# RetNet attention and a tanh-shrink MLP on one core: the first eight steps as a list of one-engine pieces, zero matmuls in TensorE's pauses, other weight pieces, and one place per chunk for the attention

## The chip, the cores and the metric

The kernel runs on one core of a Trainium2 chip. The time is the device time of one execution in microseconds (us). Five engines run beside each other, each with its own queue in order: TensorE (PE; its weight loads are PEld), VectorE (DVE), ScalarE (ACT), GpSimd (POOL) and SyncE (SP), whose queue issues nearly all DMAs here.

## The reference

```python
def _attn_ref(q, k, v):                      # each (4, 8, 768, 64) float32
    gamma = 1.0 - 2.0 ** (-5.0 - np.arange(H))
    for t in range(S):
        state = gamma * state + k[:, :, t] outer v[:, :, t]
        y[:, :, t] = scale * (q[:, :, t] @ state)

def _moe_ref(x, w_in, w_out):                # x: y as (3072, 512)
    h = x @ w_in                             # w_in (512, 2048), float64 as given
    g = h - np.tanh(h)
    return (g @ w_out).astype(np.float32)    # w_out (2048, 512), float64 as given
```

Each head keeps a 64x64 state that decays and takes in one outer product per token. The result, 3072 tokens by 512, goes through an MLP with g = h - tanh(h).

## The kernel before

*Attention.* Tokens go in 24 chunks of 128 (6 per batch). Per chunk: `load_chunk` issues three DMAs (k, q, v); `scale_chunk` multiplies q and v by powers of gamma, so that the decay needs no loop; `turn` transposes k and q on TensorE (tile `kqTp`, 4 + 4 transposes) and `turn_copy` copies them out on ScalarE; `products` computes in 64x64 pieces (tile `s`) the new state parts k^T v and the scores, and VectorE masks the scores (`a`, line 261) and adds up the states (`state`, lines 268 to 274). `outputs` then forms y from states and scores in two halves. Between the halves ScalarE copies a few elements (`seen`, line 327), a wait by which no two 64x64 pieces write one place at once; after the second half, `rest`, ScalarE copies y into `xT` (line 331).

*Weights.* They come as float64 words and are made into float32 on the chip. They are loaded and converted in 32 pieces of 0.5 MB. `convert` has two steps on ScalarE, four on VectorE (lines 172 to 178) and two on POOL (179, 183; piece 1 on VectorE). A piece of w_in covers half the rows and 256 columns, so an `up` of 256 columns needs two.

*MLP.* 96 steps (n, m2): n is a block of 256 tokens, m2 a block of 256 of the 2048 columns. `up` (tile `h`, 8 matmuls in the code, 16 in the trace, since a float32 matmul appears as two), `shrink` (five operations on ScalarE, six on VectorE, giving `g`), `down` two steps later (LAG), 4 matmuls in the code and 8 in the trace, into `o`. The first 32 steps go through the weights in quarters (f) for n = 0 to 3, the rest through n = 4 to 11 whole.

*Order.* Nothing is reordered at run time: each engine takes its instructions as the program lists them. The first four steps and eight chunks are written out by hand at the end of the function, as calls that each touch several engines. A loop over steps 4 to 95 follows. In a step with a chunk, it does `outputs` of a chunk, then `up`, then `outputs_rest` and `products` of the next chunk, `shrink`, `downs`, and `turn`. PSUM: two tiles of two banks for transposes, scores and y (tag `t`), two banks for `h`, two for `o`. k, q and v have three buffers each.

Of the kernel before, what the change touches and what calls it, by code (L numbers as in the profile page):

```python
# [31 lines left out]
def kernel(  # L32
# [51 lines left out]
    def banks(name):  # L84

        return ps.tile([P, 2, BANK], F32, tag="t", name=name)
# [10 lines left out]
    seen = cst.tile([P, 2], F32, name="seen")  # L97

# [10 lines left out]
    room = [None]  # L109
    NW = 2 * NM  # L110

    def weight_ends(i):


        f, r = divmod(i, 2 * NC)
        if r < NC:
            c, cols = 2 * (r % 2), ds(BANK * f + TH * (r // 2), TH)

            return w1[:, ds(c, 2), cols], [
                (ds(0, P), 0, w_in[ts(c, P), cols]),  # L120
                (ds(0, D), 1, w_in[ds((c + 1) * P + D, D), cols]),
                (ds(D, D), 1, w_in[ds((c + 1) * P, D), cols]),
            ]
        m = NC * f + r - NC
        return w2[:, m], w_out[ts(m, P)]

    def load_weights(i):
# [4 lines left out]
        if w_out.dtype != F32:  # L132
            if 3 <= i < 9:

                if i % 2:
                    room[0] = xp.tile([P, 2, 2 * BANK], U32, tag="xT", name=f"raws_{i}")
                raw = room[0][:, (i + 1) % 2]
            else:
                raw = stage.tile([P, 2 * BANK], U32, tag="raw", name=f"raw_{i}", bufs=3)
            raws[i] = raw  # L140
        if not isinstance(src, list):
            if raw is None:
                nc.sync.dma_start(out=dst, in_=src)
            else:
                nc.sync.dma_start(out=raw, in_=src.bitcast(U32))
            return
        for r, k, w in src:
            if raw is None:
                nc.sync.dma_start(out=dst[r, k], in_=w)
            else:  # L150
                nc.sync.dma_start(out=raw[r, ts(k, BANK)], in_=w.bitcast(U32))

    def convert(i, engine=nc.gpsimd):
# [7 lines left out]

        if i not in raws:
            return
        dst, src = weight_ends(i)
# [3 lines left out]
        power = stage.tile([P, BANK], U32, tag="power", name=f"power_{i}", bufs=1)  # L168
        low = stage.tile([P, BANK], F32, tag="low", name=f"low_{i}")
        nc.scalar.activation(head.bitcast(F32), hi.bitcast(F32), AF.Abs)  # L170
        nc.scalar.activation(low, lo, AF.Copy, scale=2.0 ** -52)
        nc.vector.tensor_scalar(head.bitcast(F32), head.bitcast(F32), HI_MIN, HI_MAX,  # L172
# [5 lines left out]
        nc.vector.tensor_scalar(power, head, 0xFF800000, None, op0=ALU.bitwise_and)  # L178
        engine.tensor_tensor(low, low, power.bitcast(F32), op=ALU.mult)  # L179
        head = head.bitcast(F32)  # L180
        if isinstance(src, list):
            low, head = (t.rearrange("p (k n) -> p k n", k=2) for t in (low, head))
        engine.tensor_tensor(dst, low, head, op=ALU.add)  # L183

# [7 lines left out]
    def load_chunk(ci):  # L192
# [4 lines left out]
        for nm, src in (("k", k), ("q", q), ("v", v)):  # L197
            t = inp.tile([P, H, D], F32, tag=nm, name=f"{nm}_{ci}")
# [3 lines left out]
    def scale_chunk(ci, engine=nc.gpsimd):  # L202
        if ci >= NCH:
            return
        j = ci % CPB
        _, qh, vh = loaded[ci]
        for t, g in ((qh, gq), (vh, gv)):
            engine.tensor_tensor(  # L208
                t, t, g[:, ts(j, H)][:, :, None].to_broadcast([P, H, D]), op=ALU.mult
            )  # L210

    def turn(ci, tag="t"):

        if ci >= NCH:
            return
        if tag == "t":
            turned[ci] = [banks(f"kqTp_{ci}")]
        else:
            turned[ci] = [bank(tag, f"kqTp{i}_{ci}")[:, None] for i in range(2)]
        to = [t[:, i] for t in turned[ci] for i in range(t.shape[1])]  # L220
        for t, tp in zip(loaded[ci], to):
            for p in range(NP):
                nc.tensor.transpose(tp[:, ts(p, P)],  # L223
                                    t[:, ds(2 * p, 2)].rearrange("p h d -> p (h d)"), ident)

    def turn_copy(ci):
        if ci >= NCH:
            return
        t = mid.tile([P, 2, NP, P], F32, tag="kqT", name=f"kqT_{ci}")
        at = 0  # L230
        for tp in turned[ci]:
            n = tp.shape[1]
            nc.scalar.copy(out=t[:, ds(at, n)], in_=tp.rearrange("p i (n t) -> p i n t", n=NP))  # L233
            at += n
        turned[ci] = t

    def products(ci):

        if ci >= NCH:
            return
        kh, _, vh = loaded[ci]
        kT, qT = (turned[ci][:, i] for i in range(2))
        sp = banks(f"s_{ci}")
        halves = sp.rearrange("p r (w n t) -> p r w n t", w=2, n=NP)
# [6 lines left out]
        for p in range(NP):  # L253
            for a in range(2):
                for i in range(2):
# [3 lines left out]
                                     skip_group_check=True)  # L259
        m = mid.tile([P, 2, NP, D], F32, tag="a", name=f"a_{ci}")  # L260
# [3 lines left out]
        masked[ci] = m  # L264
        j = ci % CPB
# [10 lines left out]

    halfway = {}

    def outputs(ci):

        j = ci % CPB
        n, nj = divmod(ci, BLK)
        if nj == 0:
            xT[n] = xp.tile([P, NP, BLK * P], F32, tag="xT", name=f"xT_{n}")
        vh = loaded.pop(ci)[2]
        qT = turned.pop(ci)[:, 1]
        a_, st = masked.pop(ci), states.pop(ci)
        yT = banks(f"y_{ci}")
        y = yT[:, :, : 2 * P].rearrange("p r (n t) -> p r n t", n=2)
        begun = set()  # L290

        def to_y(p, i, a, lhsT, rhs):

            col = (i + p) % 2
            start = (p % 2, col) not in begun
            begun.add((p % 2, col))
            nc.tensor.matmul(y[ds(D * col, D), p % 2, p // 2, ts(a, D)], lhsT, rhs,  # L297
# [20 lines left out]
        intra(True)  # L318


        flat = yT.rearrange("p r w -> p (r w)")
        for col in range(2):
            r = ds(D * col, D)
            s0, s1 = 2 * P - 1 - D, BANK + 2 * P - 1
            if col:
                s0, s1 = 2 * P - 1, BANK + 2 * P - 1 - D
            nc.scalar.copy(out=seen[r], in_=flat[r, s0 : s1 + 1 : s1 - s0])

        def rest():
            intra(False)  # L330
            nc.scalar.copy(  # L331
                out=xT[n][:, :, ts(nj, P)].rearrange("p (n r) t -> p r n t", r=2), in_=y
            )

        halfway[ci] = rest

    def outputs_rest(ci):
        halfway.pop(ci)()
# [10 lines left out]
    def up(n, m2):  # L349
        hp = bank("h", f"h_{n}_{m2}")  # L350
        for i in range(2):
            for c in range(NC):
                nc.tensor.matmul(hp[:, ts(i, TH)], w1[:, c, ts(2 * m2 + i, P)],  # L353
                                 xT[n // 2][:, c, ts(n % 2, TH)], start=(i == 0 and c == 0),
                                 stop=(c == NC - 1), skip_group_check=True)
        hps[n, m2] = hp

    def shrink(n, m2):
        hp = hps.pop((n, m2))
        u, th, large = (work(x, 2) for x in ("u", "th", "large"))  # L360
        q0, q1 = (work(x, 1) for x in ("q0", "q1"))
        nc.scalar.activation(u, hp, AF.Square)  # L362
        nc.scalar.activation(th, hp, AF.Tanh)  # L363
        nc.scalar.activation(q0, u, AF.Square, bias=bias0)  # L364
        nc.scalar.activation(q1, u, AF.Square, bias=bias1, scale=math.sqrt(A))  # L365
        nc.scalar.activation(large, u, AF.Relu, bias=bias_m)  # L366
        nc.vector.tensor_tensor(th, hp, th, op=ALU.subtract)  # L367
# [230 lines left out]
```

## Time and profile before

| | |
|---|---|
| median of 3 runs | 786.57 us (785.92 to 788.78) |
| profiled execution | 788.5 us, its span 786.7 us |
| PE busy | 758.9 us (96%) |
| DVE, ACT, POOL busy | 522.2 (66%), 370.2 (47%), 123.7 us (16%) |
| HBM read, written | 35.80 MB, 6.29 MB |

The span is the stretch from the first instruction to the last; the profiled execution's own time has 1.8 us more around it. Busy times are shares of the whole span, over a start with loads and conversions and a long stretch of matmuls alone; what limits a stretch is read from that stretch. "Idle before" is an engine's pause, with what ended it behind the arrow. The granted clock is TensorE's: 1.00 full, 0.50 half.

### The profile page before, as it was taken

The numbers are of one execution on the slowest core, as the hardware profiler recorded it, in microseconds if no ns is written. First come the engines' busy times: TensorE is split into PE (matmuls) and PEld (weight loads), VectorE is DVE, ScalarE is ACT, GpSimd is POOL, SyncE is SP. The second block draws the span as 40 slices with busy tenths as digits, with TensorE's granted clock in tenths as the row PEclk, the third lists the DMA queues.
The fourth block names the chain that finished last, engine by engine and source line by source line (L and its number), as shares of the span: only waits on it lengthen the run. The fifth ranks groups of instructions, "written<-read, shape, count | busy, mean of one in ns | idle before, by whom it ended". The sixth has DMA issues, their size and how long they took to land.

```text
span 786.7 us, 13754 instructions
## 1 busy us (share of the span) xinstructions
PE 758.9 (96%) x5504; PEld 511.9 (65%) x5504; DVE 522.2 (66%) x808; ACT 370.2 (47%) x661; POOL 123.7 (16%) x106
## 2 busy tenths in 40 slices
PE   4869999999999999999999999999999999999997
PEld 4645776677667667666666666666666666666664
DVE  4676698789888875575666565566565656655654
ACT  3453566665655654443344444344444433444432
POOL 1155354333544441000000000000000000000000
PEclk9778999999999999999999999999999999999999
DMA  9953364443433422010000000000000000000000
GB/s 203 260 123 68 87 159 118 123 110 95 120 97 95 105 45 68 29 54 1 1 27 1 0 27 1 1 27 0 13 14 1 27 1 0 27 0 1 28 0 27
DMA packets 85711, 42.97 MB, mean 55 GB/s; under 512 B 76304, under 2 KB 76432, under 8 KB 85648
## 3 DMA queue, kind: packets, MB, share of 16 engines
q1 hardware_dynamic: 85504, 41.95, 21.2%
q8 instruction: 43, 0.70, 0.4%
q10 hardware_dynamic: 144, 0.15, 0.1%
q14 instruction: 20, 0.16, 0.1%
HBM read 35.80 MB, written 6.29 MB: 54 GB/s over the span
## 4 chain that ended last, share of the span: by engine, by line
PE 92%; DVE 4%; SPq 1%; issue 1%; ACT 1%; POOL 1%; DMA 1%; DVEq 0%; POOLq 0%; ACTq 0%
PE o L385 42%; PE h L353 42%; PE y L297 3%; PE kqTp L223 2%; PE s L257 1%; PE s L251 1%; SPq L199 1%; DVE head L176 1%; DVE head L174 1%; DMA raw<-in_moe_w_in_dram 1%; DVE a L261 0%; DVE power L178 0%; POOL low L179 0%; POOL w L183 0%; DVE head L172 0%
## 5 line engine op out<-in xcount | busy, mean ns | idle before, releaser
L385 PE MATMUL o<-w,g 128*128 128x512 f32 x768 | 351.8, 601 | 5.8 <-POOL w L183 5.3
L353 PE MATMUL h<-xT,w 128*128 128x256 f32 x1536 | 354.1, 384 | 3.0 <-POOL w L183 2.2
L353 PEld LDWEIGHTS h<-xT,w 128*128 128x128 f32 x1536 | 292.4, 192 | 71.8 <-issue 31.3
L385 PEld LDWEIGHTS o<-w,g 128*128 128x128 f32 x768 | 145.4, 192 | 152.6 <-issue 138.2
L362 ACT ACTIVATE u<-h 128x512 f32<-128x512 f32 x96 | 57.4, 598 | 268.6 <-PE h L353 268.6
L367 DVE TENSOR_TENSOR th<-h,th 128x512 f32<-128x512 f32 x96 | 66.2, 690 | 159.2 <-ACT th L363 159.2
L377 DVE COPY_PREDICATED g<-large,th 128x512 f32<-128x512 int32 x96 | 73.8, 769 | 10.6 <-DVE g L376 0.9
L370 DVE SCALAR_TENSOR_TENSOR h<-q,h 128x512 f32<-128x512 f32 x96 | 66.9, 697 | 10.4 <-DVE h L368 0.5
L372 DVE SCALAR_TENSOR_TENSOR h<-q,h 128x512 f32<-128x512 f32 x96 | 66.8, 696 | 10.0
L364 ACT ACTIVATE q<-u,tab 128x512 f32<-128x512 f32 x96 | 69.5, 724 | 0.0
L365 ACT ACTIVATE q<-u,tab 128x512 f32<-128x512 f32 x96 | 69.0, 719 | 0.0
L366 ACT ACTIVATE large<-u,tab 128x512 f32<-128x512 f32 x96 | 68.8, 716 | 0.0
L376 DVE TENSOR_TENSOR g<-h,u 128x512 f32<-128x512 f32 x96 | 66.3, 691 | 3.3
L368 DVE SCALAR_TENSOR_TENSOR h<-u,h 128x512 f32<-128x512 f32 x96 | 65.8, 685 | 0.0
L179 POOL TENSOR_TENSOR low<-low,power 128x512 f32<-128x512 f32 x31 | 39.6, 1277 | 157.4 <-DVE power L178 153.7
L363 ACT ACTIVATE th<-h 128x512 f32<-128x512 f32 x96 | 57.1, 594 | 0.0
L233 ACT COPY kqT<-kqTp 128x1024 f32<-128x1024 f32 (+1 forms) x28 | 24.8, 891 | 53.2 <-PE kqTp L223 53.0
L261 DVE TENSOR_TENSOR a<-s,tab 128x512 f32<-128x512 f32 x24 | 16.6, 690 | 41.5 <-PE s L257 41.4
L183 POOL TENSOR_TENSOR w<-low,head 128x512 f32<-128x512 f32 x31 | 39.8, 1283 | 2.4
L331 ACT COPY xT<-y 128x512 f32<-128x512 f32 x24 | 14.1, 587 | 53.5 <-PE y L297 53.5
L208 POOL TENSOR_TENSOR q<-q,tab 128x512 f32<-128x512 f32 x20 | 22.3, 1115 | 14.9 <-DMA q<-in_q_dram 14.9
L297 PEld LDWEIGHTS y<-kqT,state 64*64 64x64 f32 x704 | 12.9, 134 | 17.9 <-issue 11.7
(37 smaller groups left out, 372.2 us busy)
## 6 DMA issues: line engine op xcount, KB each, us to landing
k<-in_k_dram SPq DMA_DIRECT2D x24, 256.0 KB, 4.6
q<-in_q_dram SPq DMA_DIRECT2D x24, 256.0 KB, 5.1
v<-in_v_dram SPq DMA_DIRECT2D x24, 256.0 KB, 5.4
raw<-in_moe_w_out_dram SPq DMA_DIRECT2D x12, 512.0 KB, 3.7
out_dram<-sum SPq DMA_DIRECT2D x24, 256.0 KB, 2.0
raw<-in_moe_w_in_dram SPq DMA_DIRECT2D x14, 256.0 KB, 3.0
raw<-in_moe_w_in_dram SPq DMA_DIRECT2D x28, 128.0 KB, 4.2
raws<-in_moe_w_out_dram SPq DMA_DIRECT2D x4, 512.0 KB, 5.4
```

Of the source, the lines that this page charges most:

```text
L353: nc.tensor.matmul(hp[:, ts(i, TH)], w1[:, c, ts(2 * m2 + i, P)], xT[n // 2][:, c, ts(n % 2, TH)], start=(i == 0 and c == 0), stop=(c == N ...
L362: nc.scalar.activation(u, hp, AF.Square)
L364: nc.scalar.activation(q0, u, AF.Square, bias=bias0)
L365: nc.scalar.activation(q1, u, AF.Square, bias=bias1, scale=math.sqrt(A))
L366: nc.scalar.activation(large, u, AF.Relu, bias=bias_m)
L367: nc.vector.tensor_tensor(th, hp, th, op=ALU.subtract)
L368: nc.vector.scalar_tensor_tensor(hp, in0=u, scalar=R, in1=hp, op0=ALU.subtract, op1=ALU.mult, reverse0=True)
L370: nc.vector.scalar_tensor_tensor(hp, in0=q0, scalar=C0, in1=hp, op0=ALU.add, op1=ALU.mult)
L372: nc.vector.scalar_tensor_tensor(hp, in0=q1, scalar=A * C1, in1=hp, op0=ALU.add, op1=ALU.mult)
L376: nc.vector.tensor_tensor(flat, hp, u, op=ALU.mult)
L377: nc.vector.copy_predicated(flat, large.bitcast(I32), th)
L385: nc.tensor.matmul(o_p[j], gT[n, m2][:, i, ts(j, P)], w2[:, 2 * m2 + i], start=(first and i == 0), stop=(last and i == 1))
```

## The change

1. *The first eight steps* (before: four) are one string of pieces. Each piece is one engine's part of a former call, such as `p4` (scores and state products of chunk 4 on TensorE), `m4` and `z4` (mask, states, on VectorE), `A3`, `D3`, `G3` (conversion of piece 3 on ScalarE, on VectorE, and its end on POOL, or VectorE for pieces 0 and 1), `u2` and `v2` (the two halves of step 2's up), `o2` (its down). The string also holds chunks 0 to 7 and the conversions of 12 pieces.
2. *Zeros.* `x8` says: before the next TensorE piece, 8 matmuls of a 128x128 zero tile `busy`, into the place which that piece then overwrites. 47 in all, at 11 places.
3. *w_in by 128 columns and all rows*, so that a half `up` needs one piece; rows of 1 KB in DRAM, before 2 KB. Same bytes.
4. *Chunks in the loop:* every second step from 9 to 45 (before: 4 to 31). Rest of y, products of a chunk and first half of y of another stand in one row ahead of `up`; the transposes are at the step's end as before.
5. *Buffers.* y has a tile of its own of two banks, with two chunks in its halves; tag `t` keeps one tile of two banks for two. k and q have two buffers, v four. The early raw weights take three of the `xT` buffers. `power` has two buffers for one. `see` copies four single columns in place of two pairs.

Cut to its core:

```diff
+    busy = cst.tile([P, P], F32, name="busy")
+    nc.vector.memset(busy, 0.0)
...
-            c, cols = 2 * (r % 2), ds(BANK * f + TH * (r // 2), TH)
-
-            return w1[:, ds(c, 2), cols], [
...
+            cols = ts(NC * f + r, P)
+            rows = w_in[:, cols].rearrange("(k two p) n -> p two k n", two=2, p=P)
+
+            return w1[:, :, cols], [
...
+    def keep_busy(at):
+        for _ in range(idle[0]):
+            nc.tensor.matmul(at, busy, busy, start=True, stop=True, skip_group_check=True)
+        idle[0] = 0
...
-            t = inp.tile([P, H, D], F32, tag=nm, name=f"{nm}_{ci}")
+            t = inp.tile([P, H, D], F32, tag=nm, name=f"{nm}_{ci}", bufs=4 if nm == "v" else 2)
...
+    y_banks = banks("y", "y").rearrange("p r (two n t) -> p two r n t", two=2, n=2)
...
+    BEGUN = 8
+    EARLY_TURNS = 4
+    TO_VECTOR = 2
...
+    order = """
+    L0 x8 t0 c0 s0 x5 T0 w0 L1 C0 x3 t1 W0 p0 c1 s1 m0 x2 T1 z0 W1 C1 w1 x3 b0 p1 e0 A0 r0
+    m1 z1 y0 A1 D0 L2 x4 b1 t2 e1 c2 G0 r1 s2 y1 D1 x3 T2 w2 L3 u0 C2 W2 p2 G1 s3 t3 m2 T3
+    w3 c3 v0 z2 C3 b2 A2 L4 p3 e2 W3 D2 a0 r2 s4 y2 w4 q0 W4 m3 z3 G2 x9 t4 b3 A3 d0 T4 e3
...
+    for piece in order.split():
+        pieces[piece[0]](int(piece[1:]))
...
+    with_chunk = {BEGUN + 2 * i + 1: FIRST - 3 + i for i in range(NCH - FIRST + 3)}
...
     for s in range(BEGUN, len(steps)):
...
-            scale_chunk(ci + 2)
-            outputs(ci)
...
+            if ci >= FIRST:
+                outputs_rest(ci)
+                keep_x(ci)
+            if FIRST <= ci + 2 < NCH:
+                products(ci + 2)
+                mask(ci + 2)
+                state(ci + 2)
+            load_chunk(ci + 4)
+            if FIRST <= ci + 1 < NCH:
+                outputs(ci + 1)
+                see(ci + 1)
```

What it does to the queues is shown at three places.

VectorE at the first conversion of weights (`head`, `power`, `low`), before, with the masks `a` and states of chunks 0 and 1 around it:

```order
L261 TENSOR_TENSOR a_168<-s_135,tab 128x512
L268 COPY state_170<-s_135 128x256
L274 TENSOR_TENSOR state_172<-s_135,state_170 128x256
L172 TENSOR_SCALAR head_187<-head_187 128x512
L174 TENSOR_SCALAR head_187<-head_187 128x512
L176 SCALAR_TENSOR_TENSOR head_187<-raw_104,head_187 128x512
L178 TENSOR_SCALAR power_188<-head_187 128x512
L261 TENSOR_TENSOR a_251<-s_218,tab 128x512
L270 TENSOR_TENSOR state_172<-s_218,state_172 128x256
L274 TENSOR_TENSOR state_254<-s_218,state_172 128x256
```

and now:

```order
L234 TENSOR_TENSOR v_135<-v_135,tab 128x512
L299 TENSOR_TENSOR a_273<-s_224,tab 128x512
L311 TENSOR_TENSOR state_197<-s_224,state_197 128x256
L315 TENSOR_TENSOR state_276<-s_224,state_197 128x256
L179 TENSOR_SCALAR head_261<-head_261 128x512
L181 TENSOR_SCALAR head_261<-head_261 128x512
L183 SCALAR_TENSOR_TENSOR head_261<-raw_146,head_261 128x512
L185 TENSOR_SCALAR power_284<-head_261 128x512
L193 TENSOR_TENSOR low_262<-low_262,power_284 128x512
L197 TENSOR_TENSOR w_92<-low_262,head_261 128x4x128
```

The conversion of piece 0 moved behind the states of chunk 1, and its last two operations, to `w`, came over from POOL.

TensorE around the transposes of chunk 4 (`kqTp_638`) and the second up, before:

```order
L353 MATMUL h_1_579<-xT_198,w_90 128x256 x8
L353 MATMUL h_0_629<-xT_198,w_90 128x256 x8
L223 MATMUL kqTp_638<-tab,k_329 128x128 x4
L223 MATMUL kqTp_638<-tab,q_331 128x128 x4
L385 MATMUL o_0_0_666<-w_91,g_0_576 128x512 x2
L385 MATMUL o_0_1_669<-w_91,g_0_576 128x512 x2
L251 MATMUL s_672<-v_333,k_329 64x64 x16
L257 MATMUL s_672<-kqT_647 64x64 x16
L223 MATMUL kqTp_727<-tab,k_500 128x128 x4
L223 MATMUL kqTp_727<-tab,q_502 128x128 x4
```

and now (chunk 4 is `kqTp_543`, then `s_617`):

```order
L210 MATMUL kqTp_543<-busy 128x128 x9
L248 MATMUL kqTp_543<-tab,k_463 128x128 x4
L340 MATMUL y<-kqT_425,state_432 64x64 x16
L340 MATMUL y<-a_536,v_364 64x64 x8
L248 MATMUL kqTp_543<-tab,q_465 128x128 x4
L340 MATMUL y<-a_536,v_364 64x64 x8
L210 MATMUL s_617<-busy 128x128
L286 MATMUL s_617<-v_467,k_463 64x64 x16
L292 MATMUL s_617<-kqT_596 64x64 x16
L402 MATMUL h_0_656<-xT_278,w_92 128x256 x8
L402 MATMUL h_1_680<-xT_278,w_92 128x256 x4
```

The transposes moved ahead of that up, into chunk 3's y, behind nine zero matmuls; the next up is in halves, and no down comes before chunk 4's scores.

TensorE in the loop, from one chunk's y to the next transposes, before:

```order
L297 MATMUL y_1397<-kqT_1254,state_1213 64x64 x16
L297 MATMUL y_1397<-a_1350,v_1068 64x64 x8
L353 MATMUL h_1_1437<-xT_762,w_90 128x256 x8
L297 MATMUL y_1397<-a_1350,v_1068 64x64 x8
L251 MATMUL s_1455<-v_1219,k_1215 64x64 x16
L257 MATMUL s_1455<-kqT_1393 64x64 x16
L385 MATMUL o_0_0_1378<-w_91,g_1_1235 128x512 x2
L385 MATMUL o_0_1_1381<-w_91,g_1_1235 128x512 x2
L223 MATMUL kqTp_1523<-tab,k_1355 128x128 x4
L223 MATMUL kqTp_1523<-tab,q_1357 128x128 x4
```

and now:

```order
L340 MATMUL y<-a_1670,v_1382 64x64 x8
L286 MATMUL s_2008<-v_1679,k_1675 64x64 x16
L292 MATMUL s_2008<-kqT_1948 64x64 x16
L340 MATMUL y<-kqT_1763,state_1673 64x64 x16
L340 MATMUL y<-a_1855,v_1529 64x64 x8
L402 MATMUL h_5_2093<-xT_278,w_92 128x256 x8
L450 MATMUL o_2_0_1991<-w_93,g_3_1930 128x512 x2
L450 MATMUL o_2_1_1994<-w_93,g_3_1930 128x512 x2
L248 MATMUL kqTp_2123<-tab,k_1860 128x128 x4
L248 MATMUL kqTp_2123<-tab,q_1862 128x128 x4
```

The rest of y and the products, which stood behind the up, are ahead of it, in one row with the first half of the next chunk's y.

More of the change, by code (lines that the diff above doesn't have):

```diff
@@ L226, in turn_copy @@
[L226 to L235, printed above, removed]
+        t, g = loaded[ci][1 + which], (gq, gv)[which]
+        engine.tensor_tensor(t, t, g[:, ts(ci % CPB, H)][:, :, None].to_broadcast([P, H, D]),
+                             op=ALU.mult)
@@ new lines, with turn_copy, turn_chunk @@
+    sides = {}
+    def turn_copy(ci, which=None):
+        if ci not in sides:
+            sides[ci] = mid.tile([P, 2, NP, P], F32, tag="kqT", name=f"kqT_{ci}")
+        t = sides[ci]
+        if which is None:
+            nc.scalar.copy(out=t, in_=turned[ci].rearrange("p i (n t) -> p i n t", n=NP))
+        else:
+            nc.scalar.copy(out=t[:, which],
+                           in_=turned[ci][which].rearrange("p (n t) -> p n t", n=NP))
+    def turn_chunk(ci):
+        if ci < NCH:
+            turn(ci, 0)
+            turn(ci, 1)
+            turn_copy(ci)
@@ L264, in products, with state @@
         masked[ci] = m
+    def state(ci):
+        halves = scores.pop(ci)
         j = ci % CPB
@@ L386, in down, with add_up @@
                              start=(first and i == 0), stop=(last and i == 1))
-        if not last:
-            return
+    def add_up(n, m2, j):
         done = 2 * m2 + 2 == NM
```

346 lines of the change are left out of this document (167 added, 179 removed).

## The prediction

> **What bounds the kernel now.** I read the clock and busy time by stretches first, then TensorE's waits, then the chain that ended last, then the timeline of one chunk. In the first view each row is a stretch of the span: its length, the busy time of PE, PEld, DVE, ACT and POOL (with counts), the granted clock, the DMA share and GB/s. The cuts lie where the granted clock changes. The last row is of the timeline: start, length, instruction, and in brackets the pause before it.
>
> ```profile
> 0.00:11.43 11.43, 5.70 (x80) 4.80 (x80) 2.79 (x5) 2.88 (x4) 0.20 (x4) 1.00 1.05 198
> 18.26:25.09 6.83, 4.70 (x42) 3.72 (x42) 5.76 (x9) 0.89 (x3) 0.48 (x1) 0.50 0.78 217
> 35.33:45.57 10.24, 7.50 (x47) 5.37 (x37) 8.71 (x14) 5.06 (x11) 4.34 (x4) 0.50 1.03 236
> 52.39:55.80 3.41, 0.00 (x0) 0.00 (x0) 3.15 (x6) 3.05 (x6) 1.79 (x2) 1.00 0.00 0
> 55.80:62.63 6.83, 6.02 (x28) 2.46 (x32) 2.12 (x3) 0.00 (x0) 3.21 (x3) 0.50 0.01 2
> 69.46:72.87 3.41, 1.82 (x84) 1.48 (x74) 3.31 (x6) 2.84 (x6) 2.10 (x3) 1.00 0.56 128
> 72.87:76.29 3.42, 3.42 (x5) 1.31 (x5) 3.07 (x5) 0.82 (x4) 3.42 (x4) 0.50 0.61 112
> 0.00:98.86 98.86, 75.30 (x1248) 55.39 (x1249) 62.30 (x105) 45.89 (x88) 35.20 (x34) 0.86 0.65 149
> 4.87 1.09 PE L223 MATMUL kqTp<-tab,k 128*128 128x128 f32 x4 [4.87 <-DMA k<-in_k_dram]
> ```
>
> Up to 98.86 us TensorE is busy for 75.30, so 23.6 us are pauses. Four stretches have half the clock; their busy time is 4.70 + 7.50 + 6.02 + 3.42 = 21.6 us, and the first 11.43 us, though shown as 1.00, run at half speed too (the four transposes of the last row take 1.09 us there; the same form takes 0.60 in the row of 191.75 below), with 5.70 busy: half of 27.3, 13.7 us, is lost to the clock. Half clock follows stretches of 3.4 us in which TensorE was busy for 0.00 or 1.82, and full clock came back at 76.29, after 3.42 busy of 3.42. So the start loses 37 us, and after 76 us nothing is lost. TensorE's longest waits:
>
> ```profile
> PE o L385 <- POOL w L183: 5.3, 1, 5.3
> PE kqTp L223 <- DMA k<-in_k_dram: 4.9, 1, 4.9
> PE h L353 <- POOL w L183: 2.2, 1, 2.2
> ```
>
> The second cannot go; the others are late conversions of weights. After the start TensorE is the chain itself (start, length, piece):
>
> ```profile
> 334.59 3.45 PE h L353 x16
> ...
> 706.47 3.45 PE h L353 x16
> ```
>
> 54 steps lie between: 371.88 / 54 = 6.887 us a step, 3.45 up and 3.43 down, no gap. 96 steps make 661 us that this change does not touch.
>
> **The change, step by step.** I set up the sum as: when is the order string worked off on TensorE, and what is left then.
>
> *What is left, and how the formula does on the kernel before.*
>
> ```profile
> 98.86 3.70 PE L385 MATMUL o<-w,g 128*128 128x512 f32 x8
> 182.38 0.69 PE L297 MATMUL y<-kqT,state 64*64 64x64 f32 x32
> 183.24 3.72 PE L353 MATMUL h<-xT,w 128*128 128x256 f32 x16
> 186.89 0.46 PE L297 MATMUL y<-a,v 64*64 64x64 f32 x16
> 187.17 0.65 PE L251 MATMUL s<-v,k 64*64 64x64 f32 x32
> 187.64 0.65 PE L257 MATMUL s<-kqT 64*64 64x64 f32 x32
> 188.21 3.70 PE L385 MATMUL o<-w,g 128*128 128x512 f32 x8
> 191.75 0.60 PE L223 MATMUL kqTp<-tab,k 128*128 128x128 f32 x4
> 192.62 3.62 PE L353 MATMUL h<-xT,w 128*128 128x256 f32 x16
> ...
> 199.61 0.69 PE L297 MATMUL y<-kqT,state 64*64 64x64 f32 x32
> 777.56 5.42 PE L385 MATMUL o<-w,g 128*128 128x512 f32 x12 [0.51 <-DVE g L377]
> L331 ACT COPY xT<-y 128x512 f32<-128x512 f32 x24 | 14.1, 587 | 53.5 <-PE y L297 53.5
> ```
>
> Two steps with one chunk last 199.61 - 182.38 = 17.23 us, so a chunk costs 17.23 - 13.77 = 3.46. Its own pieces are y 0.86, rest of y 0.28, s 0.47 + 0.57, transposes 0.87: 3.05. The other 0.4 is paid by the neighbours: the up between two 64x64 pieces takes 3.65 (183.24 to 186.89) where the plain one takes 3.45, and the s before a down takes 0.57 for 0.47. With rest, s and y in one row, one such pair goes: 0.20 + 0.10. I take 3.15 a chunk, 16 x 0.31 = 5 us over chunks 8 to 23. No new wait covers it up: the first y matmul stands behind ScalarE's copy of the chunk before, 0.59 us long (L331), and 0.94 us of s lies between.
>
> At 98.86 before has done 6 ups, 3 downs, chunks 0 to 7, and 1.9 us of chunk 8. Left: 90 x 6.887 + 3 x 3.43 + 15 x 3.46 + 1.5 = 683.4; the end adds 0.5 (wait for the last g) and 3.7 (782.98, where that row's last matmul ends, to 786.7): 786.5, against a span of 786.7. The formula holds.
>
> After the order string 8 ups, 6 downs and chunks 0 to 7 are done. Left: 88 x 6.887 + 2 x 3.43 + 16 x 3.15 + 4.2 = 667.5. Before reaches that much work at 98.86 + 6.9 + 10.3 - 1.9 = 114.2.
>
> *When the string is done.* I walked it piece by piece, each starting when its engine and inputs are free. Four parts result, with these rows:
>
> ```profile
> 16.86 0.42 DVE L274 TENSOR_TENSOR state<-s,state 128x256 f32<-128x256 f32 x1
> 20.38 0.69 DVE L179 TENSOR_TENSOR low<-low,power 128x512 f32<-128x512 f32 x1
> ...
> 21.72 0.69 DVE L208 TENSOR_TENSOR q<-q,tab 128x512 f32<-128x512 f32 x1
> L174 DVE TENSOR_SCALAR head<-head 128x512 uint32<-128x512 uint32 x11 | 8.5, 772 | 0.4
> L176 DVE SCALAR_TENSOR_TENSOR head<-raw,head 128x512 uint32<-128x512 uint32 x5 | 4.4, 883 | 0.2
> 29.52 0.69 DVE L261 TENSOR_TENSOR a<-s,tab 128x512 f32<-128x512 f32 x1 [4.91 <-PE s L257]
> 30.58 0.42 DVE L274 TENSOR_TENSOR state<-s,state 128x256 f32<-128x256 f32 x1
> 66.97 0.42 DVE L172 TENSOR_SCALAR head<-head 128x512 f32<-128x512 f32 x1
> 67.42 1.38 DVE L174 TENSOR_SCALAR head<-head 128x512 uint32<-128x512 uint32 x1
> 68.84 1.64 DVE L176 SCALAR_TENSOR_TENSOR head<-raws,head 128x512 uint32<-128x512 uint32 x1
> 70.58 0.43 DVE L178 TENSOR_SCALAR power<-head 128x512 uint32<-128x512 uint32 x1
> 70.92 0.68 DVE L261 TENSOR_TENSOR a<-s,tab 128x512 f32<-128x512 f32 x1
> ```
>
> (a) To the states of chunk 1. Before they end at 17.3, with a conversion (2.0 on DVE) ahead of them. After, that is behind them, but zeros stand ahead of TensorE's first pieces. A zero matmul has half the columns of an up matmul pair (2 x 0.216 for 256): 0.22 us, at half clock 0.43. The first 8 lie in the 4.9 us wait; the 5 and 3 before the next transposes cost 3.4, of which waits of 0.8 and some for k cover half. The two cancel: 17.3.
>
> (b) DVE from there to the states of chunk 3: three conversions of 0.42 + 0.77 + 0.88 + 0.43 = 2.5 (the means of L174 and L176 up to 100 us, and L172 and L178 as at 66.97 and 70.58), two endings on DVE of 1.34 (20.38 to 21.72), two masks with states of 1.5 (29.52 to 31.00): 7.5 + 2.7 + 3.0 = 13.2, and 0.7 of hand-overs: 31.2. W_in by 128 columns is what lets the up of half a tile run beside it.
>
> (c) TensorE then: 9 zeros 1.9 (they wait for the bank that these states free), transposes 0.44, y 0.86, transposes 0.6, ScalarE's copy of 1024 columns 1.0 (estimated from L331's 0.587 for 512), one zero and hand-overs 0.5: s of chunk 4 at 36.5.
>
> (d) From there TensorE always finds work: 14 half ups of 1.73 = 24.2, 6 downs 20.6, four chunks' s, y and rest 4 x 2.18 = 8.7, transposes of chunks 5 to 7 2.6, 9 zeros 1.9: 58.0. End: 94.5. DVE ends 3 us after TensorE in the walk, so it is nearly a bound itself.
>
> I add 1.5, half of the 66.97 conversion's surplus on each of two: POOL is busy 35.2 of 98.86 us before with nine endings and twelve scalings, and in the walk has ten and twelve between 17 and 80, so conversions meet it more often than the mean of 2.5 contains. 96.
>
> ```profile
> 14.00:18.00 4.00, 1.49 (x54) 0.97 (x47) 3.83 (x9) 2.27 (x6) 1.87 (x2) 1.00 1.36 217
> 46.00:48.00 2.00, 2.00 (x11) 1.77 (x10) 0.71 (x2) 1.83 (x4) 1.92 (x3) 1.00 1.03 252
> ```
>
> *What I cost at nothing.* Loads: the trace has rows of 256 B (q, k, v, at 217 GB/s) and of 2 KB (w_in, at 252), none of 1 KB. Between them a piece of 0.524 MB takes 2.08 to 2.42 us. The walk's loads run one after another: chunk 4 lands at 28 to 31, for transposes at 33, the twelfth piece at 62. Two buffers for k and q put each k load, and all behind it in SP's queue, behind TensorE's s of two chunks earlier; that is early enough by 4 us. Four small copies of ScalarE per chunk for two: ScalarE is idle half the time. The memset of zeros: in the first wait.
>
> Sum: 96 + 667.5 = 763.5 us of span. The profiled execution (788.5 us, span 786.7) lies 1.9 above the median of 786.57, so the median stands where the span does: **764**.
>
> The trace shows a conversion of 2.0 us stretched to 3.95 (66.97 to 70.92) while POOL ends the conversion before. [...]
>
> **Rivals.** *Clock not held.* Zeros and 64x64 pieces do not count enough, and TensorE runs at half clock until the first long row of ups, at some 45 us. TensorE has 22.8 us of pieces between 11.4 and that row; doubled, they add 22.8, of which its pauses of 7.5 and the shorter rest take 10: end of string 108, time 776. For: 1.82 busy of 3.41 lost the clock. Against: in the walk no 3.4 us have over 1.2 us of pause. Chance 0.12.
>
> *DVE and POOL collide.* Each conversion takes 3.95: DVE is the bound from 17 us on, 12 x 1.45 = 17 more, of which some 6 fall into slack: 107, time 774. Halfway: 769. Chance of over 770 by this: 0.10.
>
> *Nothing gained, or slower.* The same clock mechanism beyond the first ups: the string breaks ups into halves with small pieces between, so if half clock lasts to 60 us, the string ends at 115, a draw; to its end, at 135, and the time is 802. Against: full clock came back after one dense stretch of 3.42. Draw 0.03, slower 0.03.
>
> *Better.* The first zeros bring full clock at 8 instead of 11.4 us (-1.5), and POOL hits no more than now (-1.5), a chunk costs 3.05 (-1.6): 759. Chance 0.15, and the forecast itself, 760 to 769, has 0.57.
>
> [...]
>
> **How the numbers follow.** 757 to 775 leaves out 0.03 below and, above, half of the first rival (0.06), the end of the second (0.03) and the two without a gain (0.06). Under 0.5% (3.9 us) no change could be told. Faster 0.94, same 0.03, slower 0.03.
>
> **What would show it.** Right: the granted clock stays at 1.00 from about 11 us on; the PE waits of 5.3 and 2.2 on POOL are gone; the last down of the string ends near 96; up halves of chunk steps take 3.46 and a chunk step pair 16.9; DVE over 90% busy from 40 to 95. Wrong: stretches of 0.50 after 15 us, PE waiting for DVE or POOL (g or w) after 37, or conversions of 3 us and more.

## The result, and the profile after

The changed kernel takes 768.06 us (median of 4 runs, 767.69 to 769.91), the kernel before 787.25 (785.92 to 788.78): a ratio of 0.976, 95% interval 0.9735 to 0.9785. The forecast was 764, 757 to 775. The profiled execution took 768.03 us, its span is 766.0, 20.7 shorter than before.

The first view is the one by stretches, of the changed kernel, cut where the granted clock changes (columns as in the prediction). The row 36.42 to 97.72 is part (d) of the walk, and at 97.72 the first up of the loop starts, so there the string is done.

```profile
0.00:6.14 6.14, 4.93 (x22) 4.67 (x23) 0.17 (x1) 1.30 (x2) 0.20 (x4) 1.00 0.85 156
...
12.97:16.38 3.41, 1.78 (x72) 1.51 (x64) 2.49 (x6) 2.17 (x6) 0.00 (x0) 1.00 1.17 212
16.38:19.79 3.41, 3.41 (x59) 2.99 (x57) 3.24 (x5) 1.49 (x6) 1.54 (x2) 0.50 1.04 217
...
36.42:97.72 61.30, 60.20 (x700) 42.43 (x700) 55.73 (x84) 38.97 (x80) 29.92 (x24) 1.00 0.49 125
0.00:97.72 97.72, 91.53 (x1327) 70.15 (x1328) 81.04 (x125) 57.34 (x122) 39.55 (x36) 0.98 0.69 156
```

One stretch of 3.41 us has half the clock where there were four of 27.3 together, and the start runs at full clock from 6.14 instead of 11.43. Up to 97.72 TensorE pauses for 6.2 us (97.72 - 91.53); it was 23.6. TensorE's waits after:

```profile
PE kqTp L210 <- DVE state L315: 2.6, 2, 1.5
PE y L210 <- ACT xT L381: 1.5, 1, 1.5
PE kqTp L210 <- DVE busy L99: 1.1, 1, 1.1
PE y L340 <- ACT xT L381: 0.7, 1, 0.7
```

The waits of 5.3, 4.9 and 2.2 us are gone. Line 210 is the zero matmul: it is the zeros that wait now. The 4.9 us for the first k are not shorter; 1.1 of them is the memset of the zeros (`busy`), and eight zeros fill the rest.

Two steps with a chunk, in TensorE's timeline after, to be set against the rows from 182.38 in the prediction:

```profile
219.18 0.46 PE L340 MATMUL y<-a,v 64*64 64x64 f32 x16
219.46 0.65 PE L286 MATMUL s<-v,k 64*64 64x64 f32 x32
219.93 0.65 PE L292 MATMUL s<-kqT 64*64 64x64 f32 x32
220.40 0.65 PE L340 MATMUL y<-kqT,state 64*64 64x64 f32 x32
220.87 0.41 PE L340 MATMUL y<-a,v 64*64 64x64 f32 x16
221.21 3.72 PE L402 MATMUL h<-xT,w 128*128 128x256 f32 x16
224.77 3.60 PE L450 MATMUL o<-w,g 128*128 128x512 f32 x8
228.20 0.60 PE L248 MATMUL kqTp<-tab,k 128*128 128x128 f32 x4
229.07 3.62 PE L402 MATMUL h<-xT,w 128*128 128x256 f32 x16
...
236.06 0.46 PE L340 MATMUL y<-a,v 64*64 64x64 f32 x16
```

236.06 - 219.18 = 16.88 us, so a chunk costs 16.88 - 13.77 = 3.11; before it was 3.46. The down that used to stand behind s took 3.54 from start to start (188.21 to 191.75), now 3.43.

Where the time of the string went can be added up: pauses as above; the clock's loss as half of the busy time in stretches at half clock, the start included; and zeros at 0.22 us each (24 of them take 5.36 in a row further on). Before, the same work is done at 114.2 by the prediction's formula.

| us | end of string | pauses | lost to the clock | zeros | the rest |
|---|---|---|---|---|---|
| before | 114.2 | 23.6 | 13.7 | 0 | 76.9 |
| changed | 97.7 | 6.2 | 4.2 | 10.3 (47) | 77.0 |
| changed, no zeros (first experiment below) | 98.6 | 14.0 | 8.7 | 0 | 75.9 |
| changed, first 21 zeros | 96.4 | 9.4 | 5.5 | 4.6 | 76.9 |
| best version (last but one experiment) | 94.2 | 8.4 | 1.7 | 5.7 (26) | 78.4 |

The rest is TensorE's own work. It is the same in the first two rows; over all rows it differs by 2.5, so the columns are good to about that (a row of y, for one, takes 1.13 us at half clock and 0.69 at full, so it loses less than half). The change gains 17.4 us of pauses and 9.5 of clock, and pays 10.3 of zeros. After the string 766.0 - 97.7 = 668.3 us are left, 672.5 before.

### The profile page after: what moved, and what is told of

It reads as the page before. It is cut to its first block, busy times and chain, and to the rows that moved or that the text cites. A ratio compares the mean times of both kernels' runs of the same rounds, so it can differ in the third digit from the quotient of the medians.

```text
span 766.0 us, 13968 instructions
## 1 busy us (share of the span) xinstructions
PE 754.9 (99%) x5598; PEld 517.1 (68%) x5598; DVE 524.5 (68%) x807; ACT 375.3 (49%) x709; POOL 124.3 (16%) x108
## 4 chain that ended last, share of the span: by engine, by line
PE 95%; DVE 2%; SPq 1%; DMA 1%; ACT 0%; issue 0%; DVEq 0%
PE h L402 43%; PE o L450 42%; PE y L340 3%; PE kqTp L248 3%; PE s L286 1%; PE s L292 1%; SPq L227 1%; DMA raw<-in_moe_w_in_dram 1%; PE kqTp L210 0%; DVE head L183 0%; SPq L152 0%; DVE head L181 0%; PE y L210 0%; DVE power L185 0%; DVE head L179 0%
## 5 line engine op out<-in xcount | busy, mean ns | idle before, releaser
L402 PE MATMUL h<-xT,w 128*128 128x256 f32 x1536 | 349.9, 381 | 0.0
L450 PE MATMUL o<-w,g 128*128 128x512 f32 x768 | 345.5, 593 | 0.5 <-DVE g L441 0.5
L402 PEld LDWEIGHTS h<-xT,w 128*128 128x128 f32 x1536 | 288.5, 190 | 62.9 <-issue 26.5
L441 DVE COPY_PREDICATED g<-large,th 128x512 f32<-128x512 int32 x96 | 75.4, 785 | 10.9 <-DVE g L440 1.4
L234 POOL TENSOR_TENSOR q<-q,tab 128x512 f32<-128x512 f32 x22 | 23.6, 1072 | 107.6 <-DMA q<-in_q_dram 101.9
L260 ACT COPY kqT<-kqTp 128x1024 f32<-128x1024 f32 x20 | 20.2, 1012 | 22.6 <-PE kqTp L248 22.4
L340 PEld LDWEIGHTS y<-a,v 64*64 64x64 f32 x768 | 16.1, 136 | 15.0 <-ACT large L421 11.4
L234 POOL TENSOR_TENSOR v<-v,tab 128x512 f32<-128x512 f32 x22 | 24.9, 1131 | 0.8 <-DMA v<-in_v_dram 0.8
L370 ACT COPY seen<-y 64x1 f32<-64x1 f32 x96 | 10.1, 154 | 24.8 <-PE y L340 24.4
```

The costliest lines, as they stand in the source:

```text
L402: nc.tensor.matmul(hp, w1[:, c, ts(2 * m2 + i, P)], xT[n // 2][:, c, ts(n % 2, TH)], start=(i == 0 and c == 0), stop=(c == NC - 1), skip_g ...
L441: nc.vector.copy_predicated(flat, large.bitcast(I32), th)
L450: nc.tensor.matmul(o_p[j], gT[n, m2][:, i, ts(j, P)], w2[:, 2 * m2 + i], start=(first and i == 0), stop=(last and i == 1))
```

## The experiments

Three questions were open: are the zeros or the order what shortens the start, what do the 128-column pieces and the one place in the loop bring, and what still holds the string up. Each run is set against runs of the kernel before on its own chip; these had medians of 786.87 (first four), 787.65 (next three) and 787.56 us (last three). Each kernel was timed four or five times; the stretches and rows are of one execution.

### All zeros out

```diff
-    L0 x8 t0 c0 s0 x5 T0 w0 L1 C0 x3 t1 ...
+    L0 t0 c0 s0 T0 w0 L1 C0 t1 ...            # and so on for all eleven groups
```

> All 47 zero matmuls left out, the rest of the changed kernel as it is. Theory A (the zeros hold the clock, and that is where much of the gain comes from): the trace after has one half-clock stretch of 3.4 us; without zeros there are three or more, as before, full clock comes at 11 us or later in place of 6.1, and the time is 5 to 10 us longer, 773 to 778. Theory B (the order does it; the zeros mostly run after the wait they are meant to fill, since they write into the place that the next piece waits for): 9 zeros at 30.8 us, 6 at 44.1, 1 at 36.0, 3 at 60.8 and 4 at 15.9 stand in the way for 2.1 + 1.4 + 0.4 + 0.7 + 1.6 us; without them the time is within 3 us of 768, and any half-clock stretch costs no more than the zeros did.

Measured: 769.57 us, ratio 0.9771 (0.9752 to 0.979). By the medians all 47 zeros are worth 1.5 us, which is not clear of the spread (768.02 to 770.05 here, 767.69 to 769.91 with them), and the other edits keep nearly the whole gain. The stretches of this run:

```profile
18.07:24.90 6.83, 5.78 (x49) 4.68 (x49) 6.59 (x7) 2.18 (x7) 3.71 (x4) 0.50 0.70 171
35.14:38.55 3.41, 0.46 (x16) 0.32 (x16) 3.20 (x6) 2.61 (x8) 1.65 (x2) 1.00 1.04 231
38.55:41.96 3.41, 3.33 (x67) 3.00 (x68) 2.10 (x4) 1.57 (x3) 2.73 (x3) 0.50 0.99 297
```

Zeros do keep the clock (without them 10.2 us at 0.50, and full clock at 14.66 for the first time), but they take nearly the time that they save: the table's 4.5 us of clock and 7.8 of pauses against 10.3.

### Only the first five groups of zeros

```diff
-    ... L2 x4 b1 ... D1 x3 T2 ... G2 x9 t4 ... y3 x1 p4 ... L6 x6 t5 ... C7 x3 u4 ...
+    ... L2 b1 ... D1 T2 ... G2 t4 ... y3 p4 ... L6 t5 ... C7 u4 ...
```

> Only the first five groups of zeros stay (8, 5, 3, 2 and 3, up to 11.9 us); the six later groups go. Theory A (later zeros hold the clock too): half-clock stretches after 16 us, 2 to 6 us longer than the changed kernel, 770 to 774. Theory B (the later groups run after their wait and delay what follows): the 2.1 us at 30.8, 1.4 at 44.1, 0.4 at 36.0 and 0.7 at 60.8 come back, 764 to 765, full clock from 6 us on but for at most one stretch near 16 us.

Measured: 766.91 us, 0.9738 (0.9721 to 0.9755). By the medians the later 26 zeros cost about 1.2 us, less than was expected; that is hardly clear of the spread (766.18 to 767.26 here, 766.28 to 768.00 in a later repeat of the changed kernel). The rows of the changed kernel show why they do not fill a pause, TensorE first:

```profile
30.77 2.25 PE L210 MATMUL kqTp<-busy 128*128 128x128 f32 x18 [1.47 <-DVE state L315]
32.86 0.60 PE L248 MATMUL kqTp<-tab,k 128*128 128x128 f32 x4
34.87 0.46 PE L340 MATMUL y<-a,v 64*64 64x64 f32 x16
44.06 1.57 PE L210 MATMUL kqTp<-busy 128*128 128x128 f32 x12 [1.09 <-DVE state L315]
```

The nine zeros write the place that VectorE reads for the states, so they wait 1.47 us with the transposes and then delay them by 2.1. Why removing them brings so little is seen in TensorE's timeline without the later zeros, and then in ScalarE's of the changed kernel:

```profile
35.29 0.46 PE L340 MATMUL y<-a,v 64*64 64x64 f32 x16 [2.33 <-ACT seen L370]
```

```profile
33.08 0.69 ACT L170 ACTIVATE head<-raws 128x512 f32<-128x512 f32 x1 [0.94 <-DMA raws<-in_moe_w_in_dram]
...
34.38 0.43 ACT L370 COPY seen<-y 64x1 f32<-64x1 f32 x4
```

ScalarE's part of conversion 3 (lines 170, 171) stands ahead of the look at y (`seen`) in its queue and waits for its load, so y cannot go on before 34.8 with zeros or without. The zeros do stand behind their wait, but a second wait lay in their shadow.

### w_in by 256 columns again

```diff
-            cols = ts(NC * f + r, P)
-            return w1[:, :, cols], [ ...
+            c, cols = 2 * (r % 2), ds(BANK * f + TH * (r // 2), TH)
+            return w1[:, ds(c, 2), cols], [ ...
```

Since half an up then needs two pieces, `u0` was moved to just ahead of `v0` and `u1` to just ahead of `v1`; nothing else.

> Pieces of w_in as before: 256 columns and half the rows, rows of 2 KB; since a half up then needs two pieces, the first half of step 0's up moves behind the second piece's conversion and that of step 1's behind the fourth's. Theory A (the 128-column pieces matter): the first up waits for the second piece, and TensorE's pauses near 22 and 44 us grow by 1.5 to 2 us each, 770 to 772. Theory B (TensorE was waiting for VectorE's chain of conversions and masks there, not for an up): within 1.5 us of 768.

Measured: 771.83 us, 0.9801 (0.9784 to 0.9818), 3.8 more than the changed kernel; the string ends at 101.42, and what follows takes 668.3 us as in the changed kernel. The row that pays:

```profile
44.53 2.90 PE L209 MATMUL kqTp<-busy 128*128 128x128 f32 x12 [2.52 <-DVE state L314]
```

Without a half up to put there, TensorE waits 2.52 us for the states where the changed kernel waits 1.09, and a stretch at half clock follows (44.25 to 47.67). Another 0.8 us is lost before: the products of chunk 4 start at 37.20 instead of 36.42. The edit undoes the pieces and the halves together, so the 3.8 us are theirs together.

### Two places per chunk in the loop

```diff
+        # ahead of up: outputs(ci + 1), see(ci + 1) only
         up(...)
+        # behind up: outputs_rest, keep_x, products(ci + 2), mask, state, load_chunk(ci + 4)
```

> In the loop the rest of y and the products go back behind the up, as before; the order string stays. Theory A (each chunk pays for its second excursion with 0.2 us in the up and 0.1 in the products): 16 chunks x 0.3 to 0.37 = 5 to 6 us longer, 773 to 774, two steps with a chunk 17.2 us in place of 16.87. Theory B (the pairs of form changes cost nothing by themselves; the difference came from elsewhere in the loop): within 1.5 us of 768.

Measured: 773.06 us, 0.9819 (0.9801 to 0.9837), 5.0 more. The string ends at 98.05, as it should, and what follows takes 771.5 - 98.05 = 673.4 us, 5.1 more than in the changed kernel. TensorE in this run:

```profile
222.24 0.69 PE L340 MATMUL y<-kqT,state 64*64 64x64 f32 x32
...
223.09 3.72 PE L402 MATMUL h<-xT,w 128*128 128x256 f32 x16
226.75 0.46 PE L340 MATMUL y<-a,v 64*64 64x64 f32 x16
...
239.46 0.69 PE L340 MATMUL y<-kqT,state 64*64 64x64 f32 x32
```

The pair takes 17.22 us, as before the change, and the up between the two excursions 3.66 (223.09 to 226.75) where in one row it takes 3.56 (221.21 to 224.77). So the loop's part of the gain is the one excursion itself: the term of 5 us held.

### Two orders mended on ScalarE and VectorE

The kernel with the first zeros, and three moves: the look at y and the copies of chunks 3 and 4 ahead of conversion 3 on ScalarE, the states of chunk 4 ahead of conversion 4 on VectorE, `b4` ahead of `v1` on TensorE.

```diff
-    ... G2 t4 b3 A3 d0 T4 e3 C4 r3 g0 L5 y3 p4 A4 ... m4 D4 u1 G3 a2 q2 z4 L6 ... v1 W7 C5 g2 b4 s6
+    ... G2 t4 b3 d0 T4 e3 C4 r3 g0 L5 y3 p4 A3 A4 ... m4 z4 D4 u1 G3 a2 q2 L6 ... b4 v1 W7 C5 g2 s6
```

> As the kernel with only the first five groups of zeros (766.9 us), and three pieces moved in the string: the look at y, the copy of the transposes and the copy of y of chunks 3 and 4 go ahead of piece 3's conversion on ScalarE, which waits there for its load; the states of chunk 4 go ahead of piece 4's conversion on VectorE; chunk 4's first y goes ahead of the second half of step 1's up. Theory A (queue order, not the clock, is what is left to gain: TensorE's wait of 2.3 us for the look at y at 35.3, and its wait for the states at 44 in the changed kernel): the products of chunk 4 start at 34 instead of 36.4, the string ends near 92 to 93, time 762.5 to 764. Theory B (VectorE's chain is the bound of the whole string and takes back what TensorE is given): 766 to 768.

Measured: 765.57 us, 0.9721 (0.9705 to 0.9738): by the medians 1.3 us less than the kernel with the first zeros (the two intervals overlap), but short of what was expected by about as much again. ScalarE now does the look at 32.18, 2.2 earlier:

```profile
32.18 0.43 ACT L370 COPY seen<-y 64x1 f32<-64x1 f32 x4
```

The products of chunk 4 start at 33.90, where they started at 36.42 with the first zeros alone and in the changed kernel too: so it was ScalarE's order that set this time. But the string ends at 95.22, not at 92 to 93, where it ended at 96.38 with the first zeros alone: of the 2.5 us half is lost again by then. TensorE's timelines of the two runs show where. At chunk 5's transposes this run is 4.1 us ahead (40.27 for 44.35), since its products came 2.5 us earlier and the other run has a stretch at half clock there (36.44 to 39.85). Then it waits, among others, twice for work of POOL and VectorE:

```profile
42.73 1.99 PE L402 MATMUL h<-xT,w 128*128 128x256 f32 x8 [0.56 <-POOL w L197]
46.54 3.72 PE L402 MATMUL h<-xT,w 128*128 128x256 f32 x16 [0.46 <-DVE g L440]
```

A wait of 0.52 us at 51.17 ends 0.1 after VectorE's states of chunk 5, and the down from 62.94 takes 4.29 to the next start where its neighbour takes 3.64 (68.78 to 72.42). With 0.2 at 44.92 these are 2.4 of the 2.9 us lost. So both theories had a part: ScalarE's order held up chunk 4, and behind it the chain of conversions, states and `shrink` takes most of that back.

### Early scalings on VectorE

The same kernel, with the scalings of chunks 2 and 3 on VectorE in place of POOL, to see whether POOL stretches the second conversion.

```diff
-        "s": lambda c: scale(c, 0, tall(c)),
-        "w": lambda c: scale(c, 1, tall(c)),
+        "s": lambda c: scale(c, 0, nc.vector if c < 4 else nc.gpsimd),
+        "w": lambda c: scale(c, 1, nc.vector if c < 4 else nc.gpsimd),
```

> The kernel of the run before, with the scaling of q and v of chunks 2 and 3 on VectorE (4 x 0.6 us) instead of POOL. Theory A (VectorE and POOL exclude each other: the second piece's conversion took 5.85 us with its end in the changed kernel, where 3.3 is clean, because POOL scaled chunks 2 and 3): 3.2 us of stretched operations between 18.7 and 25.2 us go for 2.4 of new ones, the states of chunk 3 come 1 us earlier, 0 to 1.5 us shorter than the run before. Theory B (no exclusion; those operations are long for another reason): VectorE's chain is 2.4 us longer and the time 1.5 to 2.5 us longer than the run before.

Measured: 765.95 us, 0.9723 (0.9705 to 0.9741), no gain. The second conversion in the changed kernel, on VectorE, with POOL's scalings of the same microseconds:

```profile
18.69 1.27 DVE L179 TENSOR_SCALAR head<-head 128x512 f32<-128x512 f32 x1
19.99 1.15 DVE L181 TENSOR_SCALAR head<-head 128x512 uint32<-128x512 uint32 x1
...
21.90 1.16 DVE L185 TENSOR_SCALAR power<-head 128x512 uint32<-128x512 uint32 x1
...
30.20 0.42 DVE L315 TENSOR_TENSOR state<-s,state 128x256 f32<-128x256 f32 x1
```

```profile
18.25 1.43 POOL L234 TENSOR_TENSOR q<-q,tab 128x512 f32<-128x512 f32 x1 [17.80 <-DMA q<-in_q_dram]
19.64 1.22 POOL L234 TENSOR_TENSOR v<-v,tab 128x512 f32<-128x512 f32 x1
```

And in this run:

```profile
19.03 0.42 DVE L179 TENSOR_SCALAR head<-head 128x512 f32<-128x512 f32 x1
19.48 0.43 DVE L181 TENSOR_SCALAR head<-head 128x512 uint32<-128x512 uint32 x1
...
20.67 0.43 DVE L185 TENSOR_SCALAR power<-head 128x512 uint32<-128x512 uint32 x1
...
24.81 0.69 DVE L299 TENSOR_TENSOR a<-s,tab 128x512 f32<-128x512 f32 x1 [1.18 <-PE s L292]
...
30.41 0.42 DVE L315 TENSOR_TENSOR state<-s,state 128x256 f32<-128x256 f32 x1
```

The stretching is POOL's doing: the same instructions take 0.42 to 0.43 with POOL idle (busy for 0.00 us from 16.58 to 23.40) and 1.15 to 1.27 beside it. That the two exclude each other outright, as theory A puts it, these rows do not show. Still the states of chunk 3 end no earlier, at 30.83 for 30.62. In this run TensorE ran at half clock from 16.58 to 23.40 and the products of chunk 2 came late: VectorE has a pause of 1.18 us for them.

### The kernel before, with zeros

```diff
+    if ci == 0: zeros(...)      # 8 and 4 ahead of the first transposes
+    if ci < 6: zeros(...)       # 3 ahead of y of chunks 0 to 5
+    zeros(...)                  # 12 ahead of the second up, 25 at the first down
```

> The kernel before, with 67 zero matmuls put ahead of the pieces at which TensorE paused (8 and 4 at the first transposes, 3 ahead of y of each of chunks 0 to 5, 12 ahead of the second up, 24 ahead of the first down). Theory A (half clock is a loss of its own: 21.6 us of busy time ran at half clock after 18 us): the half-clock stretches go but for one, and the time falls by 6 to 10 us to 777 to 781. Theory B (in the old order TensorE waits for conversions and states anyway, so a faster clock turns into longer waits, and some zeros lie in the way): less than 4 us shorter, 783 to 788.

Measured: 784.48 us, 0.9957 (0.9941 to 0.9973), 3.2 less than the kernel before. Full clock comes at 6.08, but zeros alone bring little, since the long waits of that kernel are for work of others:

```profile
52.53 5.52 PE L103 MATMUL o<-busy 128*128 128x128 f32 x48
57.89 1.88 PE L400 MATMUL o<-w,g 128*128 128x512 f32 x4
```

24 zeros, 5.36 us from start to start, lie across the wait of 5.3 us in the first down, and past it the down goes on at 57.89, where the kernel before went on at 56.61. This profile is of the longest of the five executions (786.83 us): it still has one stretch of 10.24 us at half clock (33.39 to 43.63), behind the pause of 2.62 us that is shown at the end. The other four took 783.94 to 784.72.

### Both mended, zeros put ahead of chunk 2

The run with VectorE's scalings had lost its gain to the clock, so two zeros were put ahead of `t2` and three ahead of `T2`.

```diff
-    ... D0 L2 b1 t2 e1 c2 G0 r1 s2 y1 D1 T2 w2 ...
+    ... D0 L2 b1 x2 t2 e1 c2 G0 r1 s2 y1 D1 x3 T2 w2 ...
```

> The kernel with the moved pieces and the scaling of chunks 2 and 3 on VectorE, and two small groups of zeros more: 2 ahead of chunk 2's first transposes, 3 ahead of its second, both into a bank that is free before their wait ends. Theory A (that kernel lost 6.8 us of half clock from 16.6 us on to pauses of 0.6 to 0.7 us, and so gave back what the clean conversion gained): zeros that run inside the pause keep the clock, the products of chunk 2 come at 22 in place of 23.6 us, the states of chunk 3 near 29, time 763.5 to 765. Theory B (the pauses are not what decides the clock, or the states of chunk 3 hang on loads): 765 to 767.

Measured: 764.75 us, 0.9718 (0.9695 to 0.974), the shortest of all and shorter than both kernels. The clock is full from 4.37 to the end, the products of chunk 2 start at 21.92 (23.37 in the changed kernel), the states of chunk 3 end 1.1 us earlier, the string at 94.23:

```profile
21.92 0.69 PE L286 MATMUL s<-v,k 64*64 64x64 f32 x32 [0.29 <-DVE v L234]
```

```profile
29.12 0.42 DVE L315 TENSOR_TENSOR state<-s,state 128x256 f32<-128x256 f32 x1
```

Against the kernel with the mended order alone the step is 0.8 us, less than these measurements can tell; what the trace shows is the mechanism, not the size.

### The same kernels again

The changed kernel, and the one with the mended order, without any edit, to see how far the clock's stretches repeat.

> The changed kernel as it is, on the same chip as its rivals: 767.5 to 769, by every theory; the yardstick for the two others.

> The kernel with the moved pieces and the first zeros alone, again, beside the changed kernel: 765 to 766, 2 to 3 us shorter than it, if the earlier difference was the kernel's and not the chip's; the other theory (another chip) would have it within 1 us of it.

Measured: 767.73 us, 0.9746 (0.9725 to 0.9766), and 765.58, 0.9725 (0.9705 to 0.9744): the medians repeat within 0.4 us, and on this one chip the mended order is 2.1 us shorter, so that difference is the kernel's. The clock does not repeat: the changed kernel had no half clock at all this time (string done at 97.05 for 97.72), the other one 6.82 us of it where it had had none (96.33 for 95.22). So such stretches come and go without an edit, with 0.7 and 1.1 us of the string's end here, and differences of that size between single profiles show nothing.

## Why the prediction was right, and where it was off

It forecast a gain of 22.6 us on 786.57 and got 19.2 on 787.25 (787.25 - 768.06). Its mechanism held: order and half pieces take the pauses away, the clock is mostly full, and one excursion per chunk saves 0.3 us each.

- *Full clock from about 11 us on: from 6.14*, but with one stretch of 0.50 after 15 us, which was named as a sign against: a piece of the first rival, at 1.7 us instead of 12. It followed a window with 1.78 us busy, and the wait of 1.49 us for ScalarE's `xT` in it (1.5 in the waits) was not in the walk.
- *(a) states of chunk 1 at 17.3: 15.3.* The zeros and the early transposes ahead did not cancel. Without zeros these states end at 16.87 (first experiment), so the first zeros, with full clock at 6.14 instead of 14.66, are worth 1.6 of the 2.
- *(b) 13.9 to the states of chunk 3: 15.4* (30.62 - 15.26). The second conversion took 4.47 us on VectorE where 2.5 was put (the two others 2.2 and 2.3), the two endings 3.3 where 2.7 was. The scalings of chunks 2 and 3 on POOL lie beside it. It is the second rival in one place, and the 1.5 us that the prediction added for it at the end is what it cost here; (d) has a second place.
- *(c) s of chunk 4 at 36.5: 36.42.* Two errors of 2 and 1.5 us cancel, so that the number is right by luck, and a third was hidden: ScalarE's wait for a load, which had been put at nothing, set this time, not zeros and copies.
- *(d) 58.0: 61.3.* This is the term that was mis-sized. 1.1 us of it are a wait for the states of chunk 4 (44.06), where TensorE was to find work always. On VectorE these states stand behind conversion 4, which takes 4.7 us (38.30 to 43.03) beside scalings and endings on POOL: the second rival again. With the states ahead of that conversion they start at 37.46 and the wait is gone (the run with two orders mended). The other 2.2 are busy time. The walk priced every half up at 1.73 and every down at 3.43, though the prediction had seen in the loop that neighbours of 64x64 pieces take 0.1 to 0.2 longer, and the string has far more such borders. From start to start in TensorE's timeline, the 14 half ups take 25.2 for 24.2, the six downs 21.2 for 20.6, the small pieces and zeros 0.6 more than was put. Two halves of an up between small pieces take 3.66 for 3.46:

```profile
49.95 3.72 PE L402 MATMUL h<-xT,w 128*128 128x256 f32 x16
53.61 0.46 PE L340 MATMUL y<-a,v 64*64 64x64 f32 x16
```

- *Sum at 96: 97.72; left 667.5: 668.3.* The chunk's 3.15 measured 3.11, and the run with two places found 5.0 us for a term of 5. Among what is left stands 0.7 us of a wait that comes where the chunks end and no products stand between two halves of y.
- *Median at the span: off by 2.* All profiled executions here stand 1.7 to 2.1 us above their span, and the median after is 768.06 beside 768.03. The one of before lay near the top of its runs (788.5 by a median of 786.57), and by it I took off two microseconds that stand in every profile here. Of the 4 us between forecast and result this is 1.5 (763.5 had been rounded up to 764); 1.7 are the string, where (d)'s 3.3 were half covered by the 1.5 added for conversions, and 0.8 are what was left after it.
- *DVE over 90% busy from 40 to 95: 50.23 of 55.00*, 91%. *Conversions of 3 us and more would be wrong:* their mean up to 100 us is 2.9 (the five groups below), at the border, with 2.0 when alone (0.42 + 0.43 + 0.69 + 0.43 at 15.18, with POOL idle); single ones took 4.5 (from 18.69) and 4.7 us (from 38.30), so by these the sign against was there. TensorE waited for no `w` or `g` after 37 but the last `g`, 0.5 us.

```profile
L181 DVE TENSOR_SCALAR head<-head 128x512 uint32<-128x512 uint32 x12 | 9.4, 785 | 0.4
L179 DVE TENSOR_SCALAR head<-head 128x512 f32<-128x512 f32 x13 | 8.0, 616 | 0.2 <-ACT head L170 0.2
L185 DVE TENSOR_SCALAR power<-head 128x512 uint32<-128x512 uint32 x12 | 6.7, 555 | 0.4
L183 DVE SCALAR_TENSOR_TENSOR head<-raws,head 128x512 uint32<-128x512 uint32 x6 | 6.1, 1010 | 0.2
L183 DVE SCALAR_TENSOR_TENSOR head<-raw,head 128x512 uint32<-128x512 uint32 x6 | 5.1, 852 | 0.2
```

What the 19 us are made of, by the runs: one place per chunk 5.0, pieces of 128 columns (with the half ups that need them) 3.8, zeros 1.5 (not clear of the spread). Each is what the kernel loses when that part alone is taken away. The remaining 9 or so are put down to the order of the pieces with its buffers, as a difference; no run undid that alone, and nothing separates the order from the buffers.

## What to carry to other kernels

A filler is only worth its time if it can start before the wait ends: zeros that write the place for which the next piece waits stand behind that wait, and then delay it (here nine of them waited 1.47 us and then took 2.1). Before a piece is moved, read what stands behind it in the queue of its engine: a conversion that waited 0.9 us for its load held up TensorE through a copy of four elements behind it. Pieces of another shape on TensorE belong into one row, since each excursion is paid at its borders, here with 0.3 us.

## What the runs showed of the hardware

The clock. In each trace the changes of the granted clock lie whole multiples of 3.41 us apart, so it can be read window by window, here up to some 95 us of all twelve profiles. At full clock, every window with less than 1.6 us of busy TensorE was followed by half clock (0.46, 0.85, 1.18, 1.23 and 1.58 among others), and none with more than 2.1. Between these it went both ways: half clock followed 1.74, 1.78, 1.82, 1.84 and 2.05 (1.82 and 2.05 in the kernel before), and did not follow 1.69 and 1.76 (both in the kernel before with zeros), 1.86, 2.00 and 2.03. So in these traces the border lies between 1.6 and 2.1 us of the 3.41, and the busy time alone does not fix it. Full clock came back only behind windows with 3.04 us or more of busy TensorE; nine windows at half clock with 1.17 to 2.92 were followed by another.

The windows stand at a different place in each execution: one profile of the changed kernel has borders at 12.97 and 16.38 us and loses the clock behind the 1.78 us between them, the other has 11.72, 15.13 and 18.54 with 2.33 and 3.38 us busy, and keeps it. But the pauses differ as well (for `xT` 1.49 and 0.68 us), so the place alone is not shown to be the cause. Multiplying zeros counted as busy here: with zeros from 1.05 us on the clock was full at 4.1 to 6.7 us, without them at 11.43 and 14.66.

Pauses without a releaser in the profile. In the middle of rows of equal 64x64 matmuls TensorE stopped for up to 2.62 us, here in the kernel before with zeros:

```profile
33.45 1.02 PE L266 MATMUL s<-kqT 64*64 64x64 f32 x28 [2.62 <-issue]
```

Two instructions of the same row had already run at 30.55. The place goes by the number of TensorE's matmuls ahead of it. In all twelve traces a gap of 0.35 to 2.38 us from start to start stands behind the 222nd matmul record (the 221st in one), whatever that matmul is, and in the kernel before, with zeros and without, another stands behind the 476th, which is the one shown. The DMA records have a queue for instructions (`q8 instruction`, packets of 16 KB). Its first packet ends 1.4 to 1.7 us before TensorE goes on behind the 222nd in eleven of the twelve (at 17.70 for 19.10 us in the kernel before); in the twelfth TensorE waits there for a copy of ScalarE. Ahead of the two later gaps a packet ends 1.5 and 1.6 us before (31.97 for 33.45 here). So it looks like TensorE waiting for its own instructions; that is the author's inference from these times, and no run tested it. Not every "issue" is of this kind: one of 1.42 us ahead of transposes, in the runs without the later zeros, ends 0.1 us after the states of chunk 3 do.
